# One overflow condition inside a first product, in place of two between products, in a fused attention and expert kernel

## The chip, the cores and the metric

The kernel runs on one core of one Trainium2 chip. The metric is the device time of one execution in microseconds; the time of a kernel is the median of its runs.

## What is computed

Three layers run one after the other on 1792 tokens of width 768. The first is attention over 4 batches, 12 heads, 448 positions and head width 64, with normalised queries and keys. The second and the third each send every token to one of 8 experts, the one with the largest gate value, and put it through two products:

```
e_idx = np.argmax(logits, axis=1)
for e in range(E):
    mask = e_idx == e
    h = np.maximum(x[mask] @ w1[e], 0.0)          # 768 -> 1024
    out[mask] = gate_w[mask, None] * (h @ w2[e])  # 1024 -> 768
```

The second layer also multiplies by a sigmoid output gate, and the third adds a bias by modality to its logits. Both layers take their row counts per expert from the data.

## The kernel before

The attention stage fills the first third of the span and is written out by a planner. It is not touched but for one constant table. After it, everything goes in *units*. A unit is a group of at most N rows of one expert, N known when the program is built, with the number of rows really there read from a table on the chip.

**A unit** (`unit`, L375, and `halves`, L399) has two halves. In the first half there are KF=8 groups of 128 hidden columns. For each group `fb`, `split_w2(fb)` turns one 128-row tile of the second weight into a high part (a cast on ACT) and a low part (a subtraction on DVE); `mm3` (L357) issues 6 times 3 = 18 matmuls into a PSUM tile; `do(fb)` issues whatever is planned for that step; and `relu` (L362) evicts the product into `hh` on ACT and `hl` on DVE. In the second half there are KD=6 groups `db` of 8 times 3 = 24 matmuls each, evicted by ACT into `yt`, transposed by PE one group later (`pty`), scaled into `yr` by DVE, and scattered to memory by POOL. The product tiles of both halves come from one pool of three PSUM buffers (tag `pl`).

Around the products the unit prepares its successors. `nx` is the next unit, `fx` the one after it. SP loads the weights: `bring` the six tiles of the first weight (`r`), `load_w2` the eight of the second. `warm2` splits the next unit's first weight on ACT and DVE during the second half. `fetch_pay` and `fetch_rows` bring row numbers and rows of `fx` (POOL gathers them into `xr`), `xsplit` splits the rows of `nx`, and `xtrans` transposes them into `XT` by a DMA from SP. The table XPLAN and the arguments `late`, `fp`, `fr` say at which step each of these is issued. The queue of each engine is kept in exactly the order in which the program issues (`pin`).

**The order of units** after attention is: a first pair for the second layer, seven more of the second layer with 304 down to 192 rows, then `e2` and `e3` of the third layer (304 rows each), then `seq`: B0 to B3 (304 rows) and S0, S1 (128 rows).

**Overflow.** Fixed group sizes can fail to cover an uneven routing. What is left over is worked off under conditions on counts that the chip computes: `chain1` (L970) does left-over 128-row units of the second layer, and if there are any it redoes the tables and `e3`; `others` (L1000) does left-over units of the third layer. Both are nests of `tc.If`. In the profiled execution neither body runs: every engine branches past both.

A condition is a branch on each of the five engines, each comparing a register of its own. The register is loaded by each engine with `values_load` (L945 for the first condition, in the fourth of the seven units, and `known`, L1007 through L994, for the second, in S0). Behind the branch every engine has a few instructions that bring its semaphores to where the skipped body would have left them. Both conditions stand between the two halves of their unit, where `halves` yields (L411) after the eighth `relu`: the first in `e3` (`mid=mid`), the second in S1 (`mid=others`). As the bodies overwrite the unit's weights, rows and first-half results, `redo` (L445) fetches them again and repeats the first half.

For `e3` the argument `cut` also divides the loads of the next unit's first weight: three tiles before the condition, and three after it, followed later by the second weight:

```
            if warm and fb==wfb and not nx.w1: self.bring(nx,0,3 if cut else KD)
        yield
        do(7.5)
        if warm and cut: nx.e=None; self.bring(nx,3)
```

Of the kernel before, what the change touches and what calls it, by code (L numbers as in the profile page):

```python
# [27 lines left out]
class Moe:  # L28
# [251 lines left out]
    def again(self,u,v=None):  # L280
        e,u.e=u.e,None; self.fetch(u,u.slot); self.cold(u); u.e=e
        self.xall(u)
        if v is not None: self.fetch(v,v.slot)
# [93 lines left out]
    def unit(self,u,nx=None,fx=None,side=None,late=0,mid=None,fast={},now=False,fp=0,fr=7,**kw):  # L377

        gen=self.gen(); side=dict(side or {})
        plan=XPLAN[late] if nx is not None else {}  # L380
        def do(s):
            if fx is not None and s==fp: self.fetch_pay(fx)
            for k,t in plan.get(s,()):
                if t<nx.ntl:
                    if k=="t": self.xtrans(nx,t)
                    else: self.xsplit(nx,t,self.nc.gpsimd if k=="p" else None)
            if fx is not None and s==fr: self.fetch_rows(fx)
            for _ in range(fast.get(s,1)): next(gen,None)
            for f in side.pop(s,()): f()
        warm=nx is not None and not nx.same  # L390
        for _ in self.halves(u,nx,warm,do,fx,**kw):
            if mid: mid()
        for _ in gen: pass
        for s in sorted(side): do(s)
        if now:
            self.flush()
            if fx is not None: self.fetch_idx(fx)
        elif fx is not None and fr>KF+KD: self.fetch_rows(fx)
    def halves(self,u,nx,warm,do,fx=None,early=True,wfb=None,gp=0,cut=False):  # L399
# [4 lines left out]
        for fb in range(KF):  # L404
            if not u.same: self.split_w2(fb,nc.gpsimd if fb<gp else None)
            p=self.ps.tile([128,512],F32,name="pl1",tag="pl")[:,:N]
            self.mm3(p,[(self.w1h[:,k,ts(fb,128)],self.w1l[:,k,ts(fb,128)],xh[:,k],xl[:,k]) for k in range(KD)],r)
            do(fb)
            self.relu(p,hh[:,fb],hl[:,fb])
            if warm and fb==wfb and not nx.w1: self.bring(nx,0,3 if cut else KD)  # L410
        yield  # L411
        do(7.5)
        if warm and cut: nx.e=None; self.bring(nx,3)
        def w2s():
            for k in range(KF): self.load_w2(nx,k)
        if warm and not cut: w2s()
# [9 lines left out]
        for db in range(KD):  # L426
# [10 lines left out]
            if warm and cut and db==0: w2s()  # L437
# [7 lines left out]
    def redo(self,u,nx):  # L445

        e,u.e=u.e,None; self.fetch(u,u.slot); self.cold(u)
        self.xall(u)
        next(self.halves(u,None,False,lambda s: None))
        u.e=e  # L450
        if nx is not None: self.fetch(nx,nx.slot); nx.e=None; self.bring(nx,0,3); nx.e=None
# [347 lines left out]
N2=304; NE=240; CAPS=(304,288,256,240,224,208,192); G1=14; G2=10  # L799
# [6 lines left out]
def body_full(tc,q,k,v,g_q,g_k,wg,wog,w1,w2,mod,wg2,bias2,v1,v2,out,stop=False,O=None):  # L806
    nc=tc.nc
    with ExitStack() as ctx:
# [8 lines left out]
        S={}  # L817
        def early():
# [7 lines left out]
            M.set_caps(CAPS,((128,0),(N2,128)))  # L826
# [93 lines left out]
        S["s1"]=M.chunk_out("s1",G1); S["b2"]=M.chunk_out("b2",G2); S["s2"]=M.chunk_out("s2",E)  # L920
# [24 lines left out]
        def ns1(): S["NS1"]=nc.values_load(S["s1"][1][0:1,0:1],min_val=0,max_val=G1)  # L945
# [4 lines left out]
        sides={1:{KF+j:[stepper("table1")] for j in range(6)},2:{5:[stepper("pick2")]*2,**{j:[stepper("pick2")] for j in range(6,14)}},3:{2:[ns1],5:[stepper("pick3")]*2,**{j:[stepper("pick3")] for j in range(6,14)}}}  # L950
        for g in range(7): M.unit(P[g],nx=P[g+1],fx=P[g+2],side=sides.get(g),late=0 if g else 3)
        e2,e3=S["e2"],S["e3"]
        ent,ni=S["s1"]
# [16 lines left out]
        def chain1(i,NS):  # L970
            if i>=G1: return
            with tc.If(NS>i):  # L972
                u=Unit(L1,ent,i,128)
                cold(u); M.unit(u); M.flush()
                chain1(i+1,NS)
                if i==0:
                    for _ in table2(): pass
                    M.redo(e3,B0)
        def mid():
            post,M.post,sl=M.post,None,M.slot  # L980
            chain1(0,S["NS1"])
            M.slot=sl; M.post=post; B0.e=None
        t2=stepper("table2")
        M.unit(e2,nx=e3,side={j:[t2] for j in (7,8,9,10,11)})
        M.unit(e3,nx=B0,fx=S["B"][1],side={0:[lambda: M.fetch_pay(B0)],2:[lambda: M.fetch_rows(B0)]},mid=mid,cut=True,late=1,fp=8,fr=9)
# [3 lines left out]
        def more():  # L989

            a,b=[lp.tile([128,1],F32,name=n) for n in ("ova","ovb")]
            nc.vector.tensor_scalar(a,nsi,-2.0,0.0,op0=ALU.add,op1=ALU.max); nc.vector.tensor_scalar(b,nbi,-4.0,0.0,op0=ALU.add,op1=ALU.max)
            nc.vector.tensor_tensor(out=over,in0=a,in1=b,op=ALU.add)
# [6 lines left out]
        def others():  # L1000
            post,M.post,sl=M.post,None,M.slot
# [40 lines left out]
```

## Time and profile before

| what | value |
|---|---|
| median of 3 runs | 917.06 us (915.9 to 919.68) |
| the profiled execution | 913.84 us |
| its span, first to last instruction | 912.1 us |
| PE (matmul) busy | 837.5 us, 92% |
| DVE busy | 681.6 us, 75% |
| ACT busy | 526.2 us, 58% |
| POOL busy | 386.4 us, 42% |
| mean granted clock of TensorE | 0.965 of full |

The span is 1.7 us shorter than the profiled execution's own time; that execution is 3.2 us below the median. PE is TensorE's matmuls and PEld its weight loads, which overlap them. DVE, ACT and POOL are VectorE, ScalarE and GpSimd; SP issues most DMAs. A letter q behind an engine's name means its sequencer: branches, semaphore instructions, register loads. Times are from the start of the span. [...]

### The profile page before, as it was taken

The numbers are of one execution on the slowest core, as the hardware profiler recorded it, in microseconds if no ns is written. First come the engines' busy times: TensorE is split into PE (matmuls) and PEld (weight loads), VectorE is DVE, ScalarE is ACT, GpSimd is POOL, SyncE is SP. The second block draws the span as 40 slices with busy tenths as digits, with TensorE's granted clock in tenths as the row PEclk, the third lists the DMA queues.
The fourth block names the chain that finished last, engine by engine and source line by source line (L and its number), as shares of the span: only waits on it lengthen the run. The fifth ranks groups of instructions, "written<-read, shape, count | busy, mean of one in ns | idle before, by whom it ended". The sixth has DMA issues, their size and how long they took to land. (4 is left out here: it accounts for less than half of the span.)

```text
span 912.1 us, 23363 instructions
## 1 busy us (share of the span) xinstructions
PE 837.5 (92%) x8881; PEld 657.4 (72%) x8898; DVE 681.6 (75%) x1416; ACT 526.2 (58%) x967; POOL 386.4 (42%) x404
## 2 busy tenths in 40 slices
PE   4699999998998899899999999989989999999974
PEld 1365766666655688777888898987767788777864
DVE  6688888888778784777797888888656686655780
ACT  4586776776766642565455666655435554544660
POOL 5686777777766522412243232343031522402110
PEclk9799999999999899899999999999999999999996
DMA  5577666666555554987659679778647797694750
GB/s 131 124 168 186 157 158 176 166 155 167 120 150 154 131 178 134 304 232 299 190 197 318 188 246 324 242 219 303 191 146 240 251 328 192 239 269 138 273 184 8
DMA packets 143939, 181.91 MB, mean 199 GB/s; under 512 B 73737, under 2 KB 111385, under 8 KB 143809
## 3 DMA queue, kind: packets, MB, share of 16 engines
q1 hardware_dynamic: 135712, 157.45, 58.4%
q0 software_dynamic: 6784, 22.32, 7.6%
q8 instruction: 73, 1.20, 0.6%
q10 hardware_dynamic: 1312, 0.47, 0.2%
q14 instruction: 58, 0.47, 0.2%
HBM read 130.12 MB, written 24.33 MB: 169 GB/s over the span
## 5 line engine op out<-in xcount | busy, mean ns | idle before, releaser
L361 PE MATMUL pl<-XT,w1h 128*128 128x304 f16 (+7 forms) x1632 | 252.3, 263 | 2.2 <-DVE hl L365 0.9
L361 PE MATMUL pl<-hh,w2h 128*128 128x304 f16 (+7 forms) x816 | 213.7, 273 | 7.3 <-DVEq L1002 3.6
L361 PE MATMUL pl<-hh,w2l 128*128 128x304 f16 (+7 forms) x816 | 213.2, 272 | 0.0
L361 PE MATMUL pl<-XT,w1l 128*128 128x304 f16 (+7 forms) x816 | 210.0, 269 | 1.3 <-DVE w1l L299 1.3
L361 PE MATMUL pl<-hl,w2h 128*128 128x0 bf16 x816 | 206.5, 258 | 2.6 <-DVE hl L365 2.6
L361 PEld LDWEIGHTS <-w2h 128*128 128x128 f16 x1632 | 151.9, 100 | 33.0 <-ACTq L972 3.9
L361 PEld LDWEIGHTS <-w1h 128*128 128x128 f16 x1632 | 149.8, 98 | 26.3 <-issue 3.4
L652 POOL TENSOR_TENSOR plo<-p 128x448 f16<-128x448 f32 x142 | 140.3, 1006 | 50.7 <-ACT p L649 47.3
L299 DVE TENSOR_TENSOR w1l<-r,w1h 128x1024 bf16<-128x1024 f32 x96 | 116.6, 1229 | 44.1 <-ACT w1h L298 43.9
L429 ACT COPY yt<-pl 128x304 f32<-128x304 f32 (+7 forms) x102 | 37.1, 364 | 152.3 <-PE pl L361 152.3
L345 POOL TENSOR_TENSOR XS<-xr,XS 128x768 bf16<-128x768 f32 (+5 forms) x27 | 47.9, 1794 | 167.8 <-ACT XS L344 156.6
L298 ACT CAST w1h<-r 128x1024 f16<-128x1024 f32 x96 | 99.6, 1054 | 0.1
L649 ACT ACTIVATE p<-pst,eb 128x896 f32<-128x896 f32 (+1 forms) x96 | 86.4, 911 | 14.2 <-PE pst L645 13.3
L361 PEld LDWEIGHTS <-w2l 128*128 128x128 bf16 x816 | 82.0, 100 | 16.5 <-issue 3.7
L364 ACT ACTIVATE hh<-pl 128x304 f16<-128x304 f32 (+7 forms) x136 | 50.4, 373 | 73.6 <-PE pl L361 70.1
L662 PE MATMUL av<-vv,p 128*128 128x65 f16 (+1 forms) x768 | 89.2, 198 | 2.0 <-ACT xrow L674 2.0
L361 PEld LDWEIGHTS <-w1l 128*128 128x128 bf16 x816 | 80.6, 99 | 14.3 <-DVE w1l L299 1.6
L662 PEld LDWEIGHTS <-p 128*128 128x128 bf16 (+1 forms) x768 | 73.2, 102 | 20.9 <-issue 14.8
L664 PE MATMUL av<-vv,plo 128*128 128x65 f16 (+1 forms) x768 | 87.4, 195 | 0.6 <-DVE plo L652 0.6
L663 PE MATMUL av<-vv,p 128*128 128x64 f16 (+1 forms) x768 | 87.9, 197 | 0.0
L626 DVE TENSOR_REDUCE m<-psm 128x2 f16<-128x896 f32 x70 | 76.0, 1086 | 8.3 <-PE psm L621 6.5
L299 DVE TENSOR_TENSOR w2l<-raw,w2h 128x768 bf16<-128x768 f32 x64 | 73.3, 1145 | 9.1 <-ACT w2h L298 8.4
(309 smaller groups left out, 1661.0 us busy)
## 6 DMA issues: line engine op xcount, KB each, us to landing
r<-in_moe_w_dram SPq DMA_DIRECT2D x96, 512.0 KB, 8.9
raw<-in_moe_w_dram SPq DMA_DIRECT2D x64, 384.0 KB, 5.5
r2a<-in_moe_w_dram SPq DMA_DIRECT2D x32, 384.0 KB, 7.5
r2b<-in_moe_w_dram SPq DMA_DIRECT2D x32, 384.0 KB, 6.6
T<-Z SPq DMA_DIRECT2D x48, 224.0 KB, 3.5
T<-Z SPq DMA_DIRECT2D x48, 112.0 KB, 3.1
yd<-zero SPq DMA_DIRECT2D x14, 384.0 KB, 3.1
rv<-in_v_dram SPq DMA_DIRECT2D x24, 192.0 KB, 3.5
```

What stands on the lines that cost most here:

```text
L298: if part!=1: nc.scalar.copy(h,t)
L299: if part!=0: (eng or nc.vector).tensor_tensor(out=l,in0=t,in1=h,op=ALU.subtract)
L345: if part!=0: (eng or nc.vector).tensor_tensor(out=self.XS[:m,t,1].bitcast(BF16),in0=x,in1=h,op=ALU.subtract)
L361: self.nc.tensor.matmul(o,a,b,start=i==0,stop=i==tot-1); i+=1
L364: nc.scalar.activation(h,p,AF.Relu)
L429: nc.scalar.copy(self.yt[:,db,:N],p)
L626: if t<3: nc.vector.tensor_reduce(m[:,t:t+4:3],p[:,:,:S],axis=AX.X,op=ALU.max,negate=True)
L649: self.nc.scalar.activation(self.d["P",i][:,self.u(kt)],p[:,:nn,:S],AF.Exp,bias=self.eb,scale=0.125)
L652: eng.tensor_tensor(out=self.d["L",i][:,u],in0=P[:,u],in1=self.hi(P)[:,u],op=ALU.subtract)
L662: nc.tensor.matmul(o,hh,w[:,0:65],start=kt==0,stop=False)
L663: nc.tensor.matmul(o[:,0:64],hh,w[:,65:129],start=False,stop=False)
L664: nc.tensor.matmul(o,ll,w[:,0:65],start=False,stop=kt==3)
```

## The change

The two conditions become one. It is taken out of `e3` and S1 and stands in B3, the last 304-row unit (`j==3`), in the first half: behind the matmuls of group `fb`=5 (`MID`) and ahead of that group's `split_w2` and of its `relu`. That product goes to a PSUM bank of its own (`lgp`, which only the second layer uses otherwise) instead of one of the three buffers. The number that is compared, `over`, now also counts the second layer's left-over units; it is loaded in B2 at step 1 instead of in S0 at step 2, and the load for the first condition is gone. The loads of `e3`'s successor are no longer divided: all six tiles of the first weight go at step 5, and the second weight at step 7.5. The body holds the left-over units of the second layer, then third-layer units for all rows beyond those given to `e2` and `e3`, from a table with one more constant (`thr`, an iota and a cast on POOL at the start), then `redo` of B3 up to the same point. The DMAs and row splits that had been issued ahead for the next units are repeated inside the body alone. The unused function `again` is removed.

```diff
-        for _ in self.halves(u,nx,warm,do,fx,**kw):
-            if mid: mid()
+        for _ in self.halves(u,nx,warm,do,fx,cut=mid is not None,**kw): mid([k for s in plan if s<MID for k in plan[s]])
...
         for fb in range(KF):
-            if not u.same: self.split_w2(fb,nc.gpsimd if fb<gp else None)
-            p=self.ps.tile([128,512],F32,name="pl1",tag="pl")[:,:N]
+            mid=cut and fb==MID
+            if not u.same and not mid: self.split_w2(fb,nc.gpsimd if fb<gp else None)
+            p=(self.lgp if mid else self.ps.tile([128,512],F32,name="pl1",tag="pl"))[:,:N]
             self.mm3(p,[(self.w1h[:,k,ts(fb,128)],self.w1l[:,k,ts(fb,128)],xh[:,k],xl[:,k]) for k in range(KD)],r)
+            if mid: yield; self.split_w2(fb)
             do(fb)
             self.relu(p,hh[:,fb],hl[:,fb])
-            if warm and fb==wfb and not nx.w1: self.bring(nx,0,3 if cut else KD)
-        yield
+            if warm and fb==wfb and not nx.w1: self.bring(nx)
         do(7.5)
-        if warm and cut: nx.e=None; self.bring(nx,3)
         def w2s():
             for k in range(KF): self.load_w2(nx,k)
-        if warm and not cut: w2s()
+        if warm: self.expert(nx); w2s()
...
-            if warm and cut and db==0: w2s()
...
-    def redo(self,u,nx):
-
-        e,u.e=u.e,None; self.fetch(u,u.slot); self.cold(u)
-        self.xall(u)
-        next(self.halves(u,None,False,lambda s: None))
-        u.e=e
-        if nx is not None: self.fetch(nx,nx.slot); nx.e=None; self.bring(nx,0,3); nx.e=None
+    def redo(self,u,nx,fx,turn,done):
+        u.e=None; self.fetch(u,u.slot); self.cold(u); self.xall(u)
+        self.turn=turn-1; next(self.halves(u,None,False,lambda s: None,cut=True))
...
-N2=304; NE=240; CAPS=(304,288,256,240,224,208,192); G1=14; G2=10
+N2=304; NE=240; CAPS=(304,288,256,240,224,208,192); G1=14; G2=10; G4=13; MID=5
...
-            M.set_caps(CAPS,((128,0),(N2,128)))
+            M.set_caps(CAPS,((128,0),(N2,128),(N2,0)))
...
-        def ns1(): S["NS1"]=nc.values_load(S["s1"][1][0:1,0:1],min_val=0,max_val=G1)
...
-        M.unit(e3,nx=B0,fx=S["B"][1],side={0:[lambda: M.fetch_pay(B0)],2:[lambda: M.fetch_rows(B0)]},mid=mid,cut=True,late=1,fp=8,fr=9)
+        M.unit(e3,nx=B0,fx=S["B"][1],side={0:[lambda: M.fetch_pay(B0)],2:[lambda: M.fetch_rows(B0)]},late=1,fp=8,fr=9)
...
-            nc.vector.tensor_tensor(out=over,in0=a,in1=b,op=ALU.add)
+            nc.vector.tensor_tensor(out=a,in0=a,in1=b,op=ALU.add)
+            nc.vector.tensor_tensor(out=over,in0=a,in1=S["s1"][1],op=ALU.add)
...
-        def others():
-            post,M.post,sl=M.post,None,M.slot
-            with tc.If(S["over"]>0):
-                chain(load(nsi,E),2,E,lambda i: Unit(L2,se,i,128))
-                chain(load(nbi,G2),4,G2,lambda i: Unit(L2,be,i,N2))
-                M.redo(seq[-1],None)
-            M.slot=sl; M.post=post
-        def known(): S["over"]=load(over,E+G2)
-        sides={0:{KF+i:[stepper("table3")] for i in range(6)},1:{2:[more]},4:{2:[known]}}
+        def others(u,nx,fx):
+            def f(done):
+                sl,tn=M.slot,M.turn
+                assert M.post is None
+                with tc.If(S["over"]>0):
+                    ent,ni=S["s1"]
+                    chain(load(ni,G1),0,G1,lambda i: Unit(L1,ent,i,128))
+                    c=lp.tile([128,E],F32,name="c4"); M.reduce_counts(tp,c2,lp,tag="tp",out=c)
+                    rem=lp.tile([128,E],F32,name="rem"); nc.vector.tensor_tensor(out=rem,in0=c,in1=off2,op=ALU.subtract)
+                    for _ in M.chunks(S["b4"],lp,M.nchunks(lp,rem,N2,0),off2,c,N2,G4): pass
+                    be4,n4=S["b4"]
+                    chain(load(n4,G4),0,G4,lambda i: Unit(L2,be4,i,N2))
+                    M.redo(u,nx,fx,tn,done)
+                M.slot,M.turn=sl,tn; u.e=None
+                if nx is not None: nx.e=None
+            return f
+        def known(): S["over"]=load(over,E+G2+G1)
+        sides={0:{KF+i:[stepper("table3")] for i in range(6)},1:{2:[more]},2:{1:[known]}}
         for j,u in enumerate(seq):
-            M.unit(u,nx=seq[j+1] if j<5 else None,fx=seq[j+2] if j<4 else None,side=sides.get(j),late=0,mid=others if j==5 else None)
+            nx,fx=seq[j+1] if j<5 else None,seq[j+2] if j<4 else None
+            M.unit(u,nx=nx,fx=fx,side=sides.get(j),late=0,mid=others(u,nx,fx) if j==3 else None)
```

## Rows read from the trace of the kernel before

**Rows 1.** Waits of PE, whole span: us in total, times, longest.

```profile
PE pl L361 <- DVEq L1002: 3.6, 1, 3.6
PE pl L361 <- DVEq L972: 3.6, 1, 3.6
```

**Rows 2.** Instructions of the first condition's line: durations in ns min/median/max, starts in us.

```profile
L972 PEldq COMPARE_BRANCH  x1: 3952/3952/3952, 676.8 to 676.8; - x1
L972 DVEq COMPARE_BRANCH  x1: 72/72/72, 679.7 to 679.7; - x1
...
L972 DVEq EVENT_SEMAPHORE  x1: 21/21/21, 682.7 to 682.7; - x1
```

**Rows 3.** PE in order of time around the first condition: start, us, idle before.

```profile
678.95 0.29 PE L361 MATMUL pl<-XT,w1l 128*128 128x304 f16 x1
682.83 0.29 PE L361 MATMUL pl<-hh,w2h 128*128 128x304 f16 x1 [3.59 <-DVEq L972]
```

**Rows 4.** The chain that ended last, in order of time, from 600 us.

```profile
682.83 8.04 PE pl L361 x48
...
821.67 22.33 PE pl L361 x174
```

**Rows 5.** Instructions of the second condition's line, columns as in the second group.

```profile
L1002 POOLq COMPARE_BRANCH  x1: 62/62/62, 879.4 to 879.4; - x1
L1002 POOLq INC_SWDGE_SEM  x1: 2450/2450/2450, 882.7 to 882.7; - x1
L1002 PEldq COMPARE_BRANCH  x1: 3360/3360/3360, 885.0 to 885.0; - x1
```

**Rows 6.** DVE in order of time: the last eviction of the first half, S0 and S1.

```profile
868.51 0.28 DVE L365 SCALAR_TENSOR_TENSOR hl<-pl,hh 128x128 bf16<-128x128 f32 x1
...
887.81 0.28 DVE L365 SCALAR_TENSOR_TENSOR hl<-pl,hh 128x128 bf16<-128x128 f32 x1
```

**Rows 7.** ACT in order of time: second-half evictions, S0's first and three of S1.

```profile
869.17 0.27 ACT L429 COPY yt<-pl 128x128 f32<-128x128 f32 x1 [2.24 <-PE pl L361]
...
891.85 0.27 ACT L429 COPY yt<-pl 128x128 f32<-128x128 f32 x1 [5.37 <-PE pl L361]
...
895.92 0.27 ACT L429 COPY yt<-pl 128x128 f32<-128x128 f32 x1 [1.76 <-PE pl L361]
...
899.57 0.27 ACT L429 COPY yt<-pl 128x128 f32<-128x128 f32 x1 [0.95 <-PE pl L361]
```

**Rows 8.** POOL and DVE in order of time, B3's first half, groups 3 to 5.

```profile
830.15 1.39 POOL L370 DMA_INDIRECT out_dram<-yr,idx  x1 [2.31 <-DMA out_dram<-yr,idx]
...
831.41 0.47 DVE L365 SCALAR_TENSOR_TENSOR hl<-pl,hh 128x304 bf16<-128x304 f32 x1 [0.63 <-ACT hh L364]
832.13 0.96 DVE L299 TENSOR_TENSOR w2l<-r2a,w2h 128x768 bf16<-128x768 f32 x1 [0.25 <-ACT w2h L298]
```

**Rows 9.** Stretches: us, busy us of PE, PEld, DVE, ACT, POOL, granted clock, DMA share, GB/s.

```profile
564.00:568.00 4.00, 2.70 (x33) 2.55 (x31) 3.65 (x19) 1.72 (x5) 1.55 (x1) 1.00 1.05 406
...
875.50:878.50 3.00, 1.46 (x23) 1.23 (x24) 3.00 (x6) 1.24 (x4) 0.00 (x0) 0.98 1.03 409
...
878.50:880.00 1.50, 1.50 (x21) 1.50 (x19) 1.50 (x4) 0.93 (x2) 0.35 (x1) 0.50 0.55 213
```

**Rows 10.** Waits of SP's own queue, whole span: us in total, times, longest.

```profile
SPq L348 <- PE pl L361: 167.5, 12, 18.4
...
SPq L1002 <- SPq L1002: 7.2, 2, 5.5
```

**Rows 11.** SP in order of time: the weight loads of B0 in e3.

```profile
659.20 26.09 SPq L302 DMA_DIRECT2D r<-in_moe_w_dram  x6
```

**Rows 12.** DVE's register load for the second condition, in S0.

```profile
L994 DVEq TENSOR_LOAD <-over x1: 330/330/330, 861.4 to 861.4; - x1
```

**Rows 13.** POOL in order of time, start of the kernel.

```profile
12.49 0.19 POOL L40 CAST thr<-thr_128i 128x6 f32<-128x6 int32 x1
...
13.63 2.04 POOL L590 TENSOR_TENSOR qn<-raw,rs 128x512 f32<-128x512 f32 x2 [0.71 <-DMA raw<-in_k_dram]
```

More of the change, by code (lines that the diff above doesn't have):

```diff
@@ L279, in set_caps @@
         for j,n in enumerate(caps): nc.gpsimd.memset(self.caps[:,j:j+1],float(n))
-    def again(self,u,v=None):
-        e,u.e=u.e,None; self.fetch(u,u.slot); self.cold(u); u.e=e
-        self.xall(u)
-        if v is not None: self.fetch(v,v.slot)
     def alloc_state(self,st,rp):
@@ L444, in halves @@
         self.post=post
-    def redo(self,u,nx):
-        e,u.e=u.e,None; self.fetch(u,u.slot); self.cold(u)
-        self.xall(u)
-        next(self.halves(u,None,False,lambda s: None))
-        u.e=e
-        if nx is not None: self.fetch(nx,nx.slot); nx.e=None; self.bring(nx,0,3); nx.e=None
+    def redo(self,u,nx,fx,turn,done):
+        u.e=None; self.fetch(u,u.slot); self.cold(u); self.xall(u)
+        self.turn=turn-1; next(self.halves(u,None,False,lambda s: None,cut=True))
+        if nx is None: return
+        self.fetch(nx,nx.slot)
+        for k,t in done:
+            if t<nx.ntl: (self.xtrans if k=="t" else self.xsplit)(nx,t)
+        if nx.w1: nx.e=None; nx.w1=False; self.bring(nx)
+        if fx is not None: self.fetch_pay(fx,fx.slot)
     def warm2(self,db,eng):
@@ L919, in tail3 @@
             S["P"]=[Unit(L1,S["ranked"][0],g,n) for g,n in enumerate(CAPS)]
-        S["s1"]=M.chunk_out("s1",G1); S["b2"]=M.chunk_out("b2",G2); S["s2"]=M.chunk_out("s2",E)
+        S["s1"]=M.chunk_out("s1",G1); S["b2"]=M.chunk_out("b2",G2); S["s2"]=M.chunk_out("s2",E); S["b4"]=M.chunk_out("b4",G4)
         def table1():
@@ L949, in body_full @@
         P+=[LazyUnit(S,"e2"),LazyUnit(S,"e3")]
-        sides={1:{KF+j:[stepper("table1")] for j in range(6)},2:{5:[stepper("pick2")]*2,**{j:[stepper("pick2")] for j in range(6,14)}},3:{2:[ns1],5:[stepper("pick3")]*2,**{j:[stepper("pick3")] for j in range(6,14)}}}
+        sides={1:{KF+j:[stepper("table1")] for j in range(6)},2:{5:[stepper("pick2")]*2,**{j:[stepper("pick2")] for j in range(6,14)}},3:{5:[stepper("pick3")]*2,**{j:[stepper("pick3")] for j in range(6,14)}}}
         for g in range(7): M.unit(P[g],nx=P[g+1],fx=P[g+2],side=sides.get(g),late=0 if g else 3)
         e2,e3=S["e2"],S["e3"]
-        ent,ni=S["s1"]
         def cold(u): M.fetch(u); M.cold(u); M.xall(u)
@@ L969, in body_full @@
         F.update(table2=table2,table3=table3)
[L970 to L979, printed above, removed]
-            post,M.post,sl=M.post,None,M.slot
-            chain1(0,S["NS1"])
-            M.slot=sl; M.post=post; B0.e=None
         t2=stepper("table2")
         M.unit(e2,nx=e3,side={j:[t2] for j in (7,8,9,10,11)})
-        M.unit(e3,nx=B0,fx=S["B"][1],side={0:[lambda: M.fetch_pay(B0)],2:[lambda: M.fetch_rows(B0)]},mid=mid,cut=True,late=1,fp=8,fr=9)
+        M.unit(e3,nx=B0,fx=S["B"][1],side={0:[lambda: M.fetch_pay(B0)],2:[lambda: M.fetch_rows(B0)]},late=1,fp=8,fr=9)
         seq=S["B"][:4]+S["S"][:2]
@@ L999, in chain @@
                 chain(n,i+1,m,unit)
-        def others():
-            post,M.post,sl=M.post,None,M.slot
-            with tc.If(S["over"]>0):
-                chain(load(nsi,E),2,E,lambda i: Unit(L2,se,i,128))
-                chain(load(nbi,G2),4,G2,lambda i: Unit(L2,be,i,N2))
-                M.redo(seq[-1],None)
-            M.slot=sl; M.post=post
-        def known(): S["over"]=load(over,E+G2)
-        sides={0:{KF+i:[stepper("table3")] for i in range(6)},1:{2:[more]},4:{2:[known]}}
+        def others(u,nx,fx):
[16 more added lines that the diff above has]
+        sides={0:{KF+i:[stepper("table3")] for i in range(6)},1:{2:[more]},2:{1:[known]}}
         for j,u in enumerate(seq):
-            M.unit(u,nx=seq[j+1] if j<5 else None,fx=seq[j+2] if j<4 else None,side=sides.get(j),late=0,mid=others if j==5 else None)
+            nx,fx=seq[j+1] if j<5 else None,seq[j+2] if j<4 else None
+            M.unit(u,nx=nx,fx=fx,side=sides.get(j),late=0,mid=others(u,nx,fx) if j==3 else None)
         M.flush()
```

## The prediction

> **What bounds the kernel now.** I read PE's waits first, because PE is busy 92% of the span and almost every unit behind attention runs at its pace. In that list two single waits of 3.6 us stand out [rows 1]. Their releasers are the lines of the two conditions, so each is what one condition costs PE in idle time, and they are the longest waits of a product. Next I read the instructions of the first condition's line [rows 2], to see which engine is late. PE reaches its branch at 676.8, spends 3.95 us on it and is past it at 680.75. DVE reaches its own at 679.7, with the last eviction of the first half, and its next instruction stands at 682.7, 3.0 us later, although the branch itself is put down with 72 ns. PE starts again at 682.83 [rows 3], 0.13 us behind DVE. So PE waits for the last engine to pass the condition, not only for its own branch. That fits the program: the skipped body would have rewritten everything that PE reads, so PE waits for semaphore values which the other engines supply behind their branch.
>
> The third view is the chain that ended last [rows 4]. The first 48 matmuls behind the condition take 8.04 us. In B3 174 matmuls of the same width take 22.33 us, 0.128 us each, by which 48 are worth 6.16. The difference of 1.88 us is the clock: after such a gap the granted clock falls to 0.50 for a while.
>
> **What the change removes.** *In e3.* The matmul starts at 678.95 and 682.83 lie 3.88 us apart [rows 3] where 0.13 is usual: 3.75 us. With the 1.88 us of low clock [rows 4] that is **5.63 us**. Nothing takes the place of this wait: the second half needs the last eviction only in the last 3 of its first 24 matmuls, 21 times 0.128 = 2.7 us after the start, and the eviction is done within about a microsecond.
>
> *In S1.* Here a wait stays, since DVE paces the first half of S0 and S1. S0 shows how such a unit goes on without a condition: the last eviction starts at 868.51 [rows 6], the first second-half eviction at 869.17 [rows 7], 0.66 us later. S1's last eviction starts at 887.81, so its first second-half eviction should start at 888.47 instead of 891.85: 3.38 us. The next two groups take (895.92-891.85)/2 = 2.03 us each at the low clock, the last three (899.57-895.92)/3 = 1.22 [rows 7]. Without the fall the two gain 0.82 each, 1.64. Together **5.02 us**, and the kernel ends with this unit.
>
> **What it adds.** *The wait in B3.* Group 1 of the first half begins at 821.67; 72 matmuls of 0.128 us later, at 830.9, group 5 begins [rows 4], and PE has work until 833.2. DVE reaches the branch with the eviction of group 4 at 831.4 [rows 8], passes it 3.0 us later and releases PE at about 834.5: 1.3 us lost. By PE's own branch, which in e3 began with the last product (676.8; 17 matmuls before 678.95 is 676.77) and lasts 3.36 to 3.95 us [rows 2, 5], PE is ready between 834.3 and 834.9, some tenths more for its two semaphore instructions and the first weight load: 1.3 to 1.9. I take **1.6**, the middle. So the product hides 2.3 us of the stop and not all of it.
>
> [...]
>
> *The clock.* The trace has no gap of just this size. In 564 to 568 PE is idle 1.30 of 4 us and the clock stays at 1.00; in 875.5 to 878.5 it is idle 1.54 of 3 us and the following stretch runs at 0.50 [rows 9]. The nearest to 1.6 is the second, so I take a fall, at a price between the two above, 1.64 and 1.88: **1.8**. The other end is zero.
>
> **What I cost at nothing.** *Evictions and splits in B3.* Behind its branch DVE owes group 5's split and eviction, 0.96 + 0.47 = 1.43 us [rows 8], done at about 835.9, before the product of group 6 can end (834.8 + 2.3). The next group has 2.3 us for the same work. Group 5's product lies in its own bank, so groups 6 and 7 find buffers that were evicted before the condition. Without that cover up to 1.4 us would show.
>
> *POOL.* Its last scatter ahead of the condition ends at 831.54 [rows 8]. In S1 POOL needs from 879.4 to 885.15 (882.7 + 2.45) for branch and correction [rows 5], 5.75 us, so it is free at 837.3. Behind it stands the gather for S1, which is wanted a whole unit later. If PE waits for POOL, see the rivals.
>
> *SP.* Its stall at a condition is up to 5.5 us, but it waits up to 18.4 us for PE ahead of the transposes [rows 10], which is where the condition now comes. The expert number that is read again for S0 comes behind those transposes. If the cover were gone, 5.5 us would fall on loads for S0, wanted some 14 us later.
>
> *Loads in e3.* Six loads that were spread over 26.09 us, around the condition [rows 11], now go together, and the second weight goes ahead of the transposes. Both only come earlier, into time in which B0 does not need them yet, six groups of 3.4 us before B0. I expect neither gain nor loss.
>
> *Register loads and constants.* Five loads go and five move from S0 to B2. DVE's takes 0.33 us [rows 12] and stood in a half that DVE paces, so 0 to 0.33 us could be gained; I take 0, since it is the sequencer that loads, while the engine still has queued work. In B2 DVE has room (1.43 of 2.3 us used). The added iota and cast at the start are of the kind that takes 0.19 us, ahead of a POOL instruction that waits 0.71 us for a DMA [rows 13]: nothing, at most a few tenths. The one added operation for `over` is hidden likewise.
>
> **The sum.** -5.63 - 5.02 + 1.6 + 1.8 = **-7.25 us**. The profiled execution took 913.84 and would take 906.6. It lies 3.2 below the median of the runs shown, 917.06; against that median I predict **909.8**.
>
> **The rivals.** *No fall of the clock in B3.* For it: the gap lies in a stretch that is otherwise fully busy, and 1.30 idle us did no harm. Against it: the 1.54 us that did [rows 9]. It gives -9.05: 908.0.
>
> *The clock falls in S1 all the same.* PE still has to wait there for DVE's last eviction, for about a microsecond, and the gain is 1.64 smaller. S0, which waits in the same place, speaks against it. 911.4.
>
> *A slower passage.* SP's stall of 5.5 us is nearly twice DVE's 3.0 [rows 2, 10]; with 5.5 us for DVE, from 831.4 to 836.9, PE loses 3.7 and 1.8: -5.15, 911.9. [...]
>
> *PE waits for POOL.* Nothing that PE reads comes from POOL directly; if the release still hangs on it, PE starts at 837.3 and loses 4.1 and 1.8: -4.75, 912.3.
>
> *Slower than before.* The same mechanism with a longer correction on POOL. The skipped body of S1 held 12 + 36 + 1 = 49 indirect DMAs by the program, the new one 42 + 78 + 4 = 124; in proportion 2.45 us become 6.2, PE starts at 841.0 and loses 7.8 and 1.8, which leaves -1.05. It decides from a correction of about 12 us on, five times today's: then PE loses over 13.5 and the time is 921.8 or more.
>
> *The change does not do what it says* if the new condition holds; the body would then run for many units. Both old conditions were branched past [rows 2, 5], and the new number adds up the same counts, so I give this nothing.
>
> **How the numbers follow.** Forecast 0.40, no fall in B3 0.27, a fall in S1 0.12, slower passage 0.08, waiting for POOL 0.08, slower than before 0.05. The range takes in the first four, 0.87, less the runs that scatter out of it: from 908.0 down by 0.3 (a gap of 1.3), 0.33 (the load) and 1.2 (as the lowest run shown lies below its median), about 906, to 911.9 and 2 us of scatter upward, 914. Half a percent is 4.6 us, about what a measurement of this kernel can tell from no change, and lies at 912.5. Faster: the first two cases less 0.03 for scatter, and two thirds of the next three (0.28), 0.82. Slower: the last case, 0.05. The rest, 0.13, is no change.
>
> **What would show it.** Right: no wait of PE at the end of e3's or S1's first half beyond DVE's last eviction in S1; one wait of 1.3 to 1.9 us in B3, released by DVE or by PE's own branch; 0.50 in the granted clock behind it; S1's second-half evictions 1.22 us apart from the start. The forecast is wrong if B3's gap is over 3 us, if the wait in e3 turns into one for weights or rows of B0, or if S1's second half does not come about 3.4 us closer to its last eviction.

## The result, and the profile after

The changed kernel takes 906.69 us (median of 6 runs, 905.39 to 910.24); the kernel before, run beside it, takes 918.68 us (6 runs, 915.9 to 919.68). The ratio is 0.988, with an interval of 0.986 to 0.990. The time lies inside the predicted range, 3.1 us under the predicted 909.8.

The two profiled executions took 913.84 and 905.9 us, spans of 912.1 and 904.2: 7.9 us less, where the medians differ by 12.0. The profiled execution of the kernel before was faster than all six of its runs here, so its median stands 4.8 us above its profile; that of the changed kernel stands 0.8 above its own. On two other chips the kernel before took 915.14 (median of 20) and 914.54 us (median of 17), and the changed kernel, run again on the second, 905.5: 9.0 us less. Executions of one kernel lie up to 5 us from their median (910.45 to 919.9 in the 20 of the kernel before), so what a part is worth is read below within a profile, between two events of one stage.

The page, its first part, of the changed kernel: busy time, share of the span and instructions of each engine.

```profile
span 904.2 us, 23333 instructions
PE 832.4 (92%) x8881; PEld 652.0 (72%) x8898; DVE 681.5 (75%) x1417; ACT 526.9 (58%) x967; POOL 387.9 (43%) x406
```

The work is the same; PE is busy 5.1 us less with it, since fewer of its matmuls ran at the low clock (the mean granted clock is 0.974, where it was 0.965). Next the waits of PE from 640 us on (us in total, times, longest).

```profile
PE pl L357 <- DVE hl L361: 2.3, 3, 0.8
PE pl L357 <- PEq L986: 2.3, 1, 2.3
```

The two waits of 3.6 us [rows 1] are gone. One of 2.3 us on the line of the new condition (L986) has come; no other single wait is over 1.0 us. The new line's instructions (ns, first and last start in us; PE's stand under PEldq) show who is late.

```profile
L986 SPq EVENT_SEMAPHORE  x9: 17/17/17, 818.9 to 821.3; - x9
L986 POOLq EVENT_SEMAPHORE  x6: 17/30/43, 826.8 to 829.5; - x6
L986 ACTq EVENT_SEMAPHORE  x2: 17/17/17, 827.5 to 827.6; - x2
L986 DVEq EVENT_SEMAPHORE  x2: 21/21/21, 828.6 to 828.7; - x2
L986 PEldq EVENT_SEMAPHORE  x2: 51/51/51, 829.0 to 829.1; - x2
L986 SPq COMPARE_BRANCH  x1: 58/58/58, 813.5 to 813.5; - x1
L986 POOLq COMPARE_BRANCH  x1: 61/61/61, 824.2 to 824.2; - x1
L986 PEldq COMPARE_BRANCH  x1: 4212/4212/4212, 824.7 to 824.7; - x1
L986 ACTq COMPARE_BRANCH  x1: 50/50/50, 824.9 to 824.9; - x1
L986 DVEq COMPARE_BRANCH  x1: 72/72/72, 825.4 to 825.4; - x1
L986 POOLq INC_SWDGE_SEM  x1: 2380/2380/2380, 829.5 to 829.5; - x1
```

Read each engine from its branch to its first semaphore instruction: POOL 2.6 us, ACT 2.6, DVE 3.2, PE 4.2 or so, SP 5.4. The branch's own entry is short on all but PE, where it holds the whole stop. DVE is done at 828.7; PE, at its branch since 824.7, is past it at 828.9 and has its semaphores done at 829.1. PE holds itself up. POOL's last semaphore instruction, at 829.5, is no cause: in the second profile of this kernel, below, it stands at 831.0, and PE has gone on at 830.47. PE's order of time at that point (start, us, idle before):

```profile
826.88 0.29 PE L357 MATMUL lgT<-XT,w1l 128*128 128x304 f16 x1
829.51 0.41 PE L357 MATMUL pl<-XT,w1h 128*128 128x304 f16 x2 [2.34 <-PEq L986]
```

From 826.88 to 829.51 are 2.63 us where 0.13 is usual: 2.50 us lost. The stretch that begins a microsecond behind the gap (us, busy us of PE, PEld, DVE, ACT, POOL, granted clock, DMA share, GB/s):

```profile
830.60:834.00 3.40, 3.40 (x16) 1.99 (x14) 1.86 (x4) 1.12 (x3) 0.00 (x0) 0.50 0.00 0
```

Behind the gap PE runs at a granted clock of 0.50 from 830.6 to 834.0. Last, the evictions of ACT that mark the stages, in order of time: the last of the first half and the last of the second in e3, the first and the last of B3's first half, then in S1 the last of the first half and the first and last of the second.

```profile
678.65 0.42 ACT L360 ACTIVATE hh<-pl 128x304 f16<-128x304 f32 x1 [1.18 <-PE pl L357]
...
698.61 0.41 ACT L424 COPY yt<-pl 128x304 f32<-128x304 f32 x1 [2.02 <-PE pl L357]
...
815.33 0.42 ACT L360 ACTIVATE hh<-pl 128x304 f16<-128x304 f32 x1 [0.71 <-PE pl L357]
...
836.05 0.42 ACT L360 ACTIVATE hh<-pl 128x304 f16<-128x304 f32 x1 [1.62 <-issue]
...
883.18 0.28 ACT L360 ACTIVATE hh<-pl 128x128 f16<-128x128 f32 x1
885.69 0.27 ACT L424 COPY yt<-pl 128x128 f32<-128x128 f32 x1 [2.24 <-PE pl L357]
...
891.63 0.27 ACT L424 COPY yt<-pl 128x128 f32<-128x128 f32 x1 [0.94 <-PE pl L357]
```

Set against the same evictions of the kernel before, these account for the 7.9 us:

| stretch between evictions | before | after | difference |
|---|---|---|---|
| start to the last of e3's first half | 679.28 | 678.65 | -0.63 |
| e3, last of first half to last of second | 25.33 | 19.96 | -5.37 |
| from there to B3's first | 116.78 | 116.72 | -0.06 |
| B3, first half | 16.49 | 20.72 | +4.23 |
| from there to S1's first | 40.55 | 40.45 | -0.10 |
| S1, first half | 7.74 | 6.68 | -1.06 |
| S1, last of first half to last of second | 13.40 | 8.45 | -4.95 |

They add up to -7.94. The 0.63 us of the first row are there at 606 us already (606.54 and 605.91 at an eviction there), where the change has brought only one small table on POOL and the dropped register loads. They are most likely chance: up to there the two executions ran at the low clock for 41 and 34 us, partly in other stretches.

### The profile page after: what moved, and what is told of

Its sections match the earlier page's. It is cut to its first block, busy times and chain, and to the rows that moved or that the text cites. A ratio compares the mean times of both kernels' runs of the same rounds, so it can differ in the third digit from the quotient of the medians.

```text
span 904.2 us, 23333 instructions
## 1 busy us (share of the span) xinstructions
PE 832.4 (92%) x8881; PEld 652.0 (72%) x8898; DVE 681.5 (75%) x1417; ACT 526.9 (58%) x967; POOL 387.9 (43%) x406
## 5 line engine op out<-in xcount | busy, mean ns | idle before, releaser
L357 PE MATMUL pl<-XT,w1l 128*128 128x304 f16 (+7 forms) x810 | 207.9, 269 | 1.3 <-DVE w1l L295 1.3
L357 PE MATMUL pl<-hh,w2h 128*128 128x304 f16 (+7 forms) x816 | 208.5, 268 | 0.2
L357 PE MATMUL pl<-hh,w2l 128*128 128x304 f16 (+7 forms) x816 | 208.1, 267 | 0.0
L357 PE MATMUL pl<-hl,w2h 128*128 128x0 bf16 x816 | 201.6, 254 | 3.2 <-DVE hl L361 3.2
L357 PEld LDWEIGHTS <-w2h 128*128 128x128 f16 x1632 | 148.1, 98 | 24.8 <-issue 1.8
L357 PEld LDWEIGHTS <-w2l 128*128 128x128 bf16 x816 | 79.6, 98 | 17.2 <-issue 4.2
```

Source lines behind the costliest of these rows:

```text
L357: self.nc.tensor.matmul(o,a,b,start=i==0,stop=i==tot-1); i+=1
```

## The experiments

Twelve kernels, in three groups; the kernels of a group ran on one chip beside the kernel before.

**No condition at all.** The changed kernel without the condition and its body, so left-over rows would not be worked off; all else stays. It gives the floor.

```diff
-                with tc.If(S["over"]>0):
...
-                    M.redo(u,nx,fx,tn,done)
```

> The changed kernel with the condition in B3 taken out, its product still in its own bank and its split still behind the matmuls; the overflow path is left out. Theory A (a condition costs the stop of PE at its place and the low clock behind it, and nothing else): PE's wait of 2.3 us in B3 and the spell of 0.50 behind it are gone, B3's first half is 4.1 us shorter than in the changed kernel, S0 and S1 unchanged, the time about 4 us under the changed kernel (some 903 beside 907). Theory B (most of the gain comes from the loads in e3 and the register loads that were moved, a condition itself is cheap): under 1 us.

905.24 us (4 runs; before 915.14, ratio 0.988, 0.985 to 0.992). B3's first half took 16.50 us as in the kernel before, so the new condition cost 4.22 us in the profile of the changed kernel, all of it in that half. The PSUM bank and the split that comes later are free. The whole times say less: the two profiled executions have the same span, 904.2 us, since other stretches differ, and where the two kernels ran on one chip (the last group below) their medians lie 2.4 us apart and not the 4 that were expected.

**One old condition out at a time.** The kernel before, first without the condition in e3 (left-over rows of the second layer would not be worked off), with the loads still divided:

```diff
-...,mid=mid,cut=True,late=1,fp=8,fr=9)
+...,cut=True,late=1,fp=8,fr=9)
```

> The kernel before with the condition in e3 taken out and nothing else: its successor's loads are still divided, the register load for it stays; the second layer's overflow path is left out. Theory A: e3's second half begins 3.7 us earlier and without the low clock, together 5.4 to 5.6 us; the rest of the kernel keeps its times, the condition in S1 included; about 5.5 us under the kernel before. Theory B (the undivided loads bring it): e3's second half waits for the last three tiles of the next first weight, and less than 3 us is gained.

910.14 us (10 runs; ratio 0.993, 0.991 to 0.996), 5.0 us less than the kernel before. ACT in order of time, e3's last eviction of the first half and of the second:

```profile
682.06 0.42 ACT L364 ACTIVATE hh<-pl 128x304 f16<-128x304 f32 x1 [1.18 <-PE pl L361]
...
702.03 0.41 ACT L429 COPY yt<-pl 128x304 f32<-128x304 f32 x1 [1.79 <-PE pl L361]
```

That is 19.97 us, against 19.96 in the changed kernel, where the loads go together. So the condition was worth 5.36 us and the order of the loads nothing.

Then without the one in S1 (left-over rows of the third layer):

```diff
-            M.unit(...,late=0,mid=others if j==5 else None)
+            M.unit(...,late=0,mid=None)
```

> The kernel before with the condition in S1 taken out and nothing else; the third layer's overflow path is left out. Theory A: S1's second half comes 3.4 us closer to DVE's last eviction and its first two groups run at the full clock: 5 us from there to the end, 5 us under the kernel before; the low clock in S1's first half (878 to 882) stays or goes by itself, worth 1 us. Theory B (S1 waits for DVE in any case): at most 3.4 us, with the low clock staying in the second half.

911.7 us (10 runs; ratio 0.996, 0.994 to 0.997). S1's second half went from 13.40 to 8.17 us (888.57 to 896.74): 5.2 us. The first half stayed at 7.74 with the low clock at 880.8; that stretch is not the condition's doing. The median gained 3.4 us only; e3, which this kernel shares with the one before, happened to be 1.0 us slower in its profile (26.29 against 25.33), with a longer stretch at the low clock.

**Announcing the branch.** Theory: the stop is the time in which an engine gets the instructions behind the skipped body, not the comparison. An announcement (an instruction that names the branch, put ahead on the engine's queue) should then shorten it; were it the comparison, the wait for the register or the correction of the semaphores, it would change nothing. First it goes on all engines three products of B3 ahead, in the third group: by the program the branch is then 109 instructions further on PE, 11 on ACT and 8 on DVE. The first pair of lines lets the announcement be kept in its place on the queue.

```diff
-            if not on or i.engine==mybir.EngineType.Unassigned or type(i).__name__.startswith("BassTile"): continue
+            if not on or i.engine==mybir.EngineType.Unassigned or type(i).__name__.startswith("BassTile") and "Hint" not in type(i).__name__: continue
...
-                with tc.If(S["over"]>0):
+                with tc.If(S["over"]>0,label="ov"):
...
-        sides={0:{KF+i:[stepper("table3")] for i in range(6)},1:{2:[more]},2:{1:[known]}}
+        sides={0:{KF+i:[stepper("table3")] for i in range(6)},1:{2:[more]},2:{1:[known]},3:{2:[lambda: tc.mark_branch_hint_location("ov",engines=list(nc.engines))]}}
```

> The changed kernel with one more instruction on each engine three products ahead of the condition, which announces that the branch will be taken, so that the code behind it can be loaded ahead. Theory A1 (the 2.5 to 4.2 us between an engine's branch and its next instruction are the loading of the code behind the branch): PE's entry for the branch falls from 4.2 us to some tenths, ACT and DVE go on within 0.5 us, PE's wait in B3 goes from 2.3 to under 0.5 us, no low clock follows, and the time is 3.5 to 4 us under the changed kernel. Theory A2 (the engines wait for one another at the condition, or PE has to drain): the wait stays at 2 us or more.

906.29 us (5 runs; ratio 0.992, 0.989 to 0.995). The condition's line:

```profile
L986 ACTq EVENT_SEMAPHORE  x2: 17/17/17, 829.7 to 829.8; - x2
L986 DVEq EVENT_SEMAPHORE  x2: 21/21/21, 831.3 to 831.4; - x2
...
L986 PEldq COMPARE_BRANCH  x1: 419/419/419, 826.9 to 826.9; - x1
L986 ACTq COMPARE_BRANCH  x1: 68/68/68, 827.1 to 827.1; - x1
L986 DVEq COMPARE_BRANCH  x1: 84/84/84, 827.6 to 827.6; - x1
```

PE's branch fell from 4.21 to 0.42 us. ACT (2.6 us) and DVE (3.7) were not helped, and PE now waited 2.0 us for DVE. B3's first half took 18.71 us with no low clock. So half of the first theory came true: PE's branch fell as it says, but the wait stayed at the 2 us of the second, and the 3.5 to 4 us did not come. An announcement works on PE, and with PE's own branch out of the way DVE's passage is next in line. Two kernels then announced it to ACT, DVE, POOL and SP one and two units earlier, PE's staying where it was: at the first step of B2 (shown) and of B1.

```diff
+        def hint_at(es): tc.mark_branch_hint_location("ov",engines=es)
+        ET=mybir.EngineType
+        sides.setdefault(2,{}).setdefault(0,[]).append(lambda: hint_at([ET.Activation,ET.DVE,ET.Pool,ET.SP]))
+        sides.setdefault(3,{}).setdefault(2,[]).append(lambda: hint_at([ET.PE]))
```

> The same with the announcement one unit ahead (in B2) on ACT, DVE, POOL and SP, some 60 to 80 instructions. Theory A1: as the run before, PE waits under 0.6 us in B3 and its first half takes 16.5 to 17.1 us; if only the longer distance works, this one shows where it begins. Theory A3: 18.5 us or more.

> The changed kernel with the announcement of the branch two units ahead (in B1) on ACT, DVE, POOL and SP, and three products ahead on PE as in the earlier run, where PE's entry fell to 0.42 us while ACT and DVE, which had it 8 to 11 instructions ahead, still needed 2.6 and 3.7 us. Theory A1 (ACT and DVE got it too late in instructions): over 100 instructions ahead, they go on within 0.5 us of their branch, PE waits under 0.6 us in B3, and B3's first half (first to last eviction) is 16.5 to 17.1 us, beside 20.7 in the changed kernel and 16.5 without the condition. Theory A3 (on these engines the announcement does nothing): 2.5 us and more as before, B3's first half 18.5 or more.

One execution each: 909.74 and 910.19 us (before 921.64). In both ACT's and DVE's passages fell to 0.5 to 0.7 us, PE's wait to 0.6 and B3's first half to 17.26 us, with no low clock. SP (4.5 to 4.8 us) and POOL (2.8 to 2.9) were not helped and held nothing up. The times of these single executions do not show the gain: those of this group differ by up to 4.6 us before e3 ends. That one unit ahead:

```profile
L986 ACTq EVENT_SEMAPHORE  x2: 17/17/17, 832.8 to 832.8; - x2
L986 DVEq EVENT_SEMAPHORE  x2: 21/21/21, 833.3 to 833.4; - x2
L986 PEldq EVENT_SEMAPHORE  x2: 51/51/51, 834.6 to 834.7; - x2
...
L986 PEldq COMPARE_BRANCH  x1: 414/414/414, 832.1 to 832.1; - x1
L986 ACTq COMPARE_BRANCH  x1: 68/68/68, 832.3 to 832.3; - x1
L986 DVEq COMPARE_BRANCH  x1: 84/84/84, 832.7 to 832.7; - x1
```

Now PE, ACT and DVE are through by 833.4, well inside the product. PE's semaphore instructions still stand only at 834.6, behind its last matmul, and the 0.6 us that is left lies around them.

That the stop is a fetch can be read more directly, since the profiles also hold the DMA packets that bring instructions. Over 25 us around the condition q14, one of the two queues that carry them, has ten packets in the changed kernel (810 to 835 us) and six in the announced one (813 to 838); with no condition (810 to 835) it has none (queue: packets, MB, share of 16 engines).

```profile
q14 instruction: 10, 0.08, 1.0%
...
q14 instruction: 6, 0.05, 0.6%
```

The other, q8, has one packet of 16 KB inside PE's branch, from 824.7 to 828.9 in the changed kernel:

```profile
q8 instruction: 1, 0.02, 1.6%
```

It starts 1.6 us behind the branch's start, takes 1.1 us, and 1.5 us later the branch is over. All eight branches of PE in these profiles that were not announced hold such a packet: it starts 1.0 to 1.8 us behind the branch's start, takes 0.9 to 1.2, and 1.4 to 1.6 us follow to the branch's end. Those that went through in 0.41 to 0.43 us hold none. So PE's stop is the wait for that fetch, and its spread from 3.4 to 4.4 us is mostly that of the moment at which the fetch starts; what delays it stays open. For ACT and DVE the profile does not say which packet is whose, and the effect of the announcement is the evidence.

**Where in the product the condition stands.** In the same group of runs, the split of the second weight ahead of the condition (DVE comes to its branch later), and the condition behind the eviction of its own product:

```diff
-            if not u.same and not mid: self.split_w2(...)
+            if not u.same: self.split_w2(...)
...
-            if mid: yield; self.split_w2(fb)
+            if mid: yield
```

> The changed kernel with the split of the sixth tile of the second weight ahead of the condition again instead of behind it. DVE then reaches the branch about 0.6 to 0.7 us later. Theory P (PE is held by its own branch, 4.2 us, and DVE is past earlier): PE's wait in B3 grows by at most 0.4 us, from 2.3 to 2.7 at most. Theory D (PE is held by DVE, as at the two old conditions): it grows by the whole 0.6 to 0.7 us.

```diff
-            if not u.same and not mid: self.split_w2(...)
+            if not u.same: self.split_w2(...)
...
-            if mid: yield; self.split_w2(fb)
             do(fb)
             self.relu(p,hh[:,fb],hl[:,fb])
+            if mid: yield
```

> The changed kernel with the condition behind the eviction of its product, between two products as the old ones were: the product no longer lies between the branch of ACT and DVE and the next product of PE. Theory A (what hides part of the stop is that all engines branch while this product still runs): DVE reaches its branch 2.3 us later and PE waits 3.6 to 3.8 us as at the old conditions, 1.4 more than in the changed kernel, B3's first half 22.1 us. Theory B (the place inside the unit hides nothing, the gain is that there is one condition less): unchanged, 2.3 us and 20.7.

One execution each, 907.27 and 910.05 us. In the first, DVE took from 829.7 to 832.6 and PE waited 1.9 us for it; B3's first half took 18.58 us with no low clock. Neither expected growth of the wait came, it shrank; and the run does not say which engine holds PE in the changed kernel, since PE's branch was shorter this time (3.49 us). In the second PE's longest wait is that at the condition; the wait, then the condition's line:

```profile
PE pl L357 <- DVEq L986: 3.5, 1, 3.5
```

```profile
L986 DVEq EVENT_SEMAPHORE  x2: 21/21/21, 833.7 to 833.8; - x2
...
L986 DVEq COMPARE_BRANCH  x1: 72/72/72, 830.8 to 830.8; - x1
```

DVE reaches its branch only when the product has been evicted, and its 2.9 us stand bare. B3's first half took 21.88 us, 1.2 more than in the first profile of the changed kernel, 3.5 more than in its second (below), and 5.4 more than with no condition: what each old condition cost. So one condition less is not the whole of the gain; the place inside the product brings these 1.2 to 3.5 us, what the clock does behind the gap included.

**Four kernels on one chip.** The announcement of one unit ahead, the changed kernel itself, the kernel before with both its branches announced in the same manner (e2's first step for the first, S0's for the second, PE's in the fifth group of the unit itself), and no condition.

> The changed kernel with the branch announced one unit ahead on ACT, DVE, POOL and SP and three products ahead on PE, as in the look before, now timed. Theory A1 (the stop at the condition is the loading of the code behind the branch): PE waits about 0.6 us in B3, its first half takes 17.3 us, no low clock behind it, the time is 3 to 4 us under the changed kernel's on the same chip and under 1 us above the kernel without any condition. Theory A3 (chance of one execution): no difference to the changed kernel.

> The changed kernel again, beside the others on the same chip: B3's first half 20 to 21 us with a wait of PE of 1.9 to 2.5 us, 8 to 12 us under the kernel before. The time of the code loading on PE has been seen between 3.4 and 4.2 us, so the wait should vary by as much.

> The kernel before with both branches announced in the same way, the conditions where they were. Theory A1: PE's two waits of 3.6 us fall to about 1.3 us in e3 and to DVE's last eviction plus 0.7 us in S1, no low clock follows, so e3's second half ends 4 us and S1's about 4.5 us earlier, 8 to 9 us under the kernel before in all: loading, not the place, is the larger part of what a condition costs. Theory P (the place is what counts): the waits stay above 2.5 us and less than 4 us is gained in all.

> The changed kernel without the condition (the overflow path left out) again, timed beside the others: 4 us under the changed kernel, 0.8 us under the one with the announcement, the floor for what can be done about the condition.

| kernel | median us (runs) | ratio to before, interval | B3's first half, us |
|---|---|---|---|
| before | 914.54 (17) | | |
| changed, announced | 904.92 (6) | 0.989, 0.986 to 0.991 | 17.26 |
| changed | 905.5 (6) | 0.991, 0.989 to 0.993 | 18.37 |
| before, both announced | 913.57 (12) | 0.999, 0.996 to 1.001 | 16.50 |
| changed, no condition | 903.12 (6) | 0.989, 0.986 to 0.991 | 16.50 |

The changed kernel did not repeat its own gap. Waits of PE in B3, the condition's line, PE's first matmul behind it, and the stretch around the gap (granted clock third from the end):

```profile
PE pl L357 <- DVEq L986: 1.7, 1, 1.7
```

```profile
L986 POOLq EVENT_SEMAPHORE  x6: 17/30/43, 828.4 to 831.0; - x6
...
L986 DVEq EVENT_SEMAPHORE  x2: 21/21/21, 830.3 to 830.4; - x2
...
L986 PEldq COMPARE_BRANCH  x1: 3537/3537/3537, 826.4 to 826.4; - x1
```

```profile
830.47 0.42 PE L357 MATMUL pl<-XT,w1h 128*128 128x304 f16 x2 [1.66 <-DVEq L986]
```

```profile
829.00:832.00 3.00, 1.53 (x12) 1.20 (x13) 0.62 (x1) 1.49 (x3) 0.00 (x0) 1.00 0.05 15
```

PE's branch took 3.54 us, DVE was last, PE lost 1.9 us, and the clock stayed at 1.00, in the four microseconds behind it too. So the new condition cost 4.2 us of B3 in the one profile and 1.9 in the other. Announced, it cost 0.8, in all three profiles. By the medians on this chip the condition costs 2.4 us, announced 1.8, and the 0.6 us between the two is less than the runs scatter: the announcement shows in the profile, and as a gain of the whole, of which 3 to 4 us were expected, it is not shown.

In the kernel before the announcement failed to pay: 1.0 us by the medians, with no change inside the interval, where 8 to 9 were expected. The two conditions' lines:

```profile
L972 PEldq COMPARE_BRANCH  x1: 429/429/429, 676.8 to 676.8; - x1
L972 ACTq COMPARE_BRANCH  x1: 68/68/68, 679.3 to 679.3; - x1
L972 DVEq COMPARE_BRANCH  x1: 84/84/84, 679.8 to 679.8; - x1
L972 DVEq EVENT_SEMAPHORE  x1: 21/21/21, 680.4 to 680.4; - x1
...
L972 ACTq EVENT_SEMAPHORE  x1: 17/17/17, 681.9 to 681.9; - x1
```

```profile
L1004 ACTq EVENT_SEMAPHORE  x2: 17/17/17, 885.0 to 885.1; - x2
L1004 DVEq EVENT_SEMAPHORE  x2: 21/21/21, 885.7 to 885.8; - x2
...
L1004 PEldq COMPARE_BRANCH  x1: 1470/1470/1470, 881.4 to 881.4; - x1
L1004 ACTq COMPARE_BRANCH  x1: 54/54/54, 882.4 to 882.4; - x1
L1004 DVEq COMPARE_BRANCH  x1: 74/74/74, 882.7 to 882.7; - x1
```

At the first condition PE (0.43 us) and DVE (0.6) pass quickly, but ACT needs 2.6 us as if it had not been told, and PE waits 2.7 for ACT. At the second ACT (2.6) and DVE (3.0) were not helped and PE only partly (1.47), and PE waits 3.5. For PE the packets suggest why: the last one of 16 KB starts 1.3 us ahead of the branch and lands inside it, and the branch ends 1.3 us later; in the other announced profiles the last had landed 2.5 to 4.3 us ahead. The three products between announcement and branch begin 1.07 us apart in S1, with 128 rows, and 2.3 in B3, so PE was most likely told too late. In this profile e3's stretch still shrank from 25.33 to 22.74 us, mostly because no low clock came behind the gap, and S1's second half from 13.40 to 12.13; the median shows nothing of it. One engine that is late keeps the wait. Both waits stayed above 2.5 us, which is what the theory of the place said, but not for its reason, as the announcement had not taken everywhere. Why it did not take on ACT and DVE stays open: it lay 65 to 124 instructions ahead there by the program, and 63 and 78 where it worked.

## Why the prediction was right

**What was removed: right to within 0.3 us.** The sum had -5.63 for e3 and -5.02 for S1's second half. Measured were -5.37 and -4.95, and with one old condition out at a time -5.36 and -5.2. There is no new wait and no low clock in either place in the profile of the changed kernel. S1's second half begins 2.51 us behind its last first-half eviction (883.18 to 885.69) where it was 5.68, so it came 3.2 us closer, 3.4 being forecast, and its evictions stand 1.1 to 1.2 us apart from the start.

**The wait in B3: the term that was mis-sized.** The step took 1.6 us, the middle of 1.3 (DVE) and 1.3 to 1.9 (PE's own branch). The profile gave 2.50, with PE's own branch as the holder. The construction was right: PE's branch began at 824.7 with the product of its group, and PE has work to 827.0. But the branch took 4.21 us where the rows of before offered 3.36 and 3.95 [rows 2, 5], and from its end (828.91) to the first matmul (829.51) another 0.6 went by, of which the "some tenths more" had allowed 0.2. In the second profile of the same kernel PE's branch took 3.54, DVE held PE, and the loss was 1.9. In all profiles without an announcement PE's branch took 3.4 to 4.4 us and DVE's passage 2.9 to 3.3: the two end close together, and which is last changes.

What the branch's own entry shows is not the price of passing a condition: in the profile of the changed kernel it took 50 to 72 ns on ACT, SP, POOL and DVE, and their passages took 2.6 to 5.4 us. On PE, where the entry holds the whole stop, a packet of instructions lies inside each branch that was not announced, and an announcement brings PE's branch from 4.21 to 0.42 us and DVE's passage from 3.2 to 0.6.

**The clock in B3: right in one profile, wrong in the other.** The 1.8 us were 1.7 (4.23 less 2.50) in the first, and 0 in the second. The prediction took the nearest gap in the trace of before and let it decide. The gaps at a condition in the runs are more telling: PE idle 0.6, 1.7, 1.9, 2.0 and 2.7 us with the clock at 1.00 behind it, and 2.3, 3.5, 3.6 and 3.8 us with 0.50 soon after. A gap of 2.7 us did no harm and one of 2.3 did, so the length of the gap alone doesn't settle it. That the fall came in the first of the two profiles is luck; the forecast and its first rival (no fall, 0.27) were one case with an uncertain term.

**What was left out.** S1's first half took 6.68 instead of 7.74 us: the low clock at 878.5 [rows 9] was not there. That is 1.06 us which the sum didn't have, and the change didn't make it: the kernel without S1's condition kept 7.74, as did the changed kernel without a condition, and other runs of either kind had 6.48. It is chance, as the 0.63 ahead of e3 most likely is.

**What was costed at nothing was nothing.** B2's half, B3's second half and S0 did not change (-0.06 and -0.10 in the table): SP's 5.4 us, POOL's branch, the loads in one piece and the moved register load are all hidden. The correction on POOL took 2.38 us, not the 6.2 of the rival by which the kernel would have been slower, although the body has two and a half times the indirect DMAs; and it began at 829.5, when PE went on, so PE did not wait for it either, nor for POOL's semaphore instructions, as the second profile shows.

**From the sum to the median.** The sum was -7.25, the spans differ by 7.9: 0.7 us. The other 2.4 of the 3.1 us by which the forecast was too high come from adding the 3.2 us that lay between the profiled execution of before and its median. For the changed kernel that distance was 0.8. So the terms were better than the total shows, in part by luck: the wait was 0.9 too small, and the two chance gains of 1.06 and 0.63 stood against it. What the sum does not give is the gain by the medians of the two kernels side by side, 12.0 us on this chip and 9.0 on the other, both more than 7.25. The profiled execution of the kernel before lies below all six of its runs here, and which stretches make the rest in the others no profile shows.

## What to carry to other kernels

In these profiles a skipped condition cost PE what the last of the engines it waited for needed to get past it, its own passage included (in the second profile of the changed kernel it went on at 830.47, with DVE's last semaphore instruction at 830.4), so measure per engine from the branch to its next instruction, not by the branch's entry (on DVE 2.9 to 3.3 us where the entry says 63 to 72 ns). Put the condition where the engine that sets the pace has the most work already issued: inside a product, with the eviction behind the branch, it cost 1.9 and 4.2 us in two profiles, behind the eviction 5.4 in one. An announcement of the branch, early on all engines, lowered the cost inside the product to 0.8 in three profiles, with no gain shown in the medians. Look in the profile whether each engine took it, as one that did not kept the wait: ACT at the first condition of the kernel before, 2.7 us.

## What the runs showed of the hardware

At the taken branches of these kernels most of the stop went on PE, ACT and DVE once the engine had been told of the branch early enough: on PE 3.4 to 4.4 us without the announcement and 0.41 to 0.43 with it, on DVE 2.9 to 3.3 against 0.6 or so, on ACT 2.6 against 0.5. On PE the stop was the wait for a fetch: a packet of 16 KB of instructions that starts 1.0 to 1.8 us into the branch lies inside each of the eight that were not announced, and in none of those that took 0.41 to 0.43 us. An announcement 8 instructions ahead on DVE and 11 on ACT did not help (3.7 and 2.6 us); one more than 60 ahead did in the changed kernel (0.5 to 0.7) and did not always in the kernel before (ACT 2.6 at both conditions, DVE 3.0 at the second). On PE one three products ahead served where these took 6.9 us (0.41 to 0.43), and only partly where they took about 3 (1.47). With PE, ACT and DVE through their branches, PE still lost 0.7 us: its semaphore instructions stood behind the end of its product (831.3, where the last matmul began at 830.97), so it went on with a gap. POOL's correction took 1.94 to 2.47 us in all profiles; with two and a half times the indirect DMAs in the body by the program it took 2.38, against 2.45 and 2.47 at the old condition in S1.
